# A list scheduler inside a kernel gets other numbers for its clock: engine overlap, bank release and matmul cadence in an attention and gated-unit kernel

## The chip, the core and the metric

The kernel runs on one core of one Trainium2 chip. The time is the device time of that core in microseconds, from the first to the last instruction and what lies around them; the document compares medians of several executions. The engines are called as the profile calls them: PE (TensorE matmul), PEld (its weight loads), DVE (VectorE), ACT (ScalarE), POOL (GpSimd), SP (SyncE, which issues most DMAs).

## What is computed

The input x has 2048 tokens of 576 features, in fp32. Cut to what matters:

```python
xn = _layernorm(x)
# A: attention, 32 heads of 18 features
qkv = xn @ wqkv;  q, k, v = per head
s = softmax(q @ k.T * 18 ** -0.5) @ v   # per head
s = concat(s) @ wo
# B: gated unit, 4608 columns, no nonlinearity inside
h = (xn @ w_gate) * (xn @ w_up)
g = silu(h @ w_down)
out = x + s * g
```

## The kernel before

**Three stages.** A first stage normalises x, turns it to columns and computes q, k and v. A main stage does the attention of all 32 heads and the gated unit at the same time. An end stage multiplies the attention output by wo, multiplies by the gate and adds x. The change touches the main stage only.

**Two halves of the array.** In the main stage PE's 128 rows are used as two halves of 64 rows that run different matmuls at once; the code calls them r = 0 and r = 1, and here they are half 0 and half 1. fp32 values are split into a high and a low part, so each product takes several matmuls. Five kinds of matmul are mixed:

- `a_item` (line 541), 64 per head, almost all on half 0: a 128x512 block of scores, written to one of two PSUM banks "a". DVE takes the row maximum of it (line 543). Below: an A.
- `b_item` (line 580), 64 per head, almost all on half 1: the block of scores again, transposed, with the maximum already inside, into one of two banks "b". ACT takes the exponential (line 582). Below: a B.
- `gu_op` (line 629): half 0 sums 27 matmuls into an up projection, which ACT copies out (line 636); half 1 sums 27 into a gate projection, which DVE multiplies by it (line 643). ACT and POOL then split the product (646, 653).
- `down_op` (line 677): half 0 puts three 128x288 matmuls into a bank, half 1 three more into the same bank, so the bank is handed over from one half to the other. DVE adds the sum to an accumulator (line 734), or ACT copies it out (728) and POOL adds it (697).
- `pv_group` (line 591): probabilities times v, in full fp32 over all 128 rows and four column strips. It needs both halves. It comes 96 times, three times a head, for 5, 5 and 6 blocks of tokens, and DVE or ACT empties its bank (597, 595). After a head's third group DVE finishes the head (`finish`, lines 605 to 609), and after every second head SP stores it (line 614).

Up, gate, down and `pv_group` share four banks "g". Below, a **stretch** is the work that both halves do between two `pv_group`s: 97 stretches in all. A half that has come to the end of its list in a stretch waits there for the other, since the next `pv_group` takes both.

**What sets the order.** Nothing in the order is decided at run time: each engine executes its instructions in the order in which they were written, and waits on semaphores where data or a bank is not ready. The order is made when the program is built, by the list scheduler `order()`. It keeps a clock per half (`clk`), the time from which each other engine is free (`free`, advanced by `engine()`), and the time from which each bank is free (`banks`). It takes the half whose clock is behind and issues an A or a B if its bank is free by this clock and its due time (`a_goal`, `b_goal`) has come, otherwise a down or an up or gate matmul whose data and bank are ready (`pick`, `can_go`). If nothing is ready it lets that half's clock run on by up to 0.3 and tries again; no instruction is written for such idle time. `visit()` writes a `pv_group` when enough exponentials are due and the two clocks stand within 0.04 of each other, or after 1.0 of waiting. The due times follow from `pace`, which is worked out from `part` and `span` ahead of the scheduler. `small()` slips in the splitting of weights, and the silu of finished tokens, when an engine is free.

Two details matter for the end of the main stage: the down matmuls of the last unit use a tile `wdl`, and `can_go` lets a unit's down matmuls begin only when `downed` of the unit before has passed, a time that `moved()` makes from the length of a DMA.

Of the kernel before, what the change touches and what calls it, by code (L numbers as in the profile page):

```python
# [40 lines left out]
def kernel(  # L41
# [456 lines left out]
    n = 8  # L498
# [24 lines left out]
    with ExitStack() as mid:  # L523
# [168 lines left out]
        def by_act(u, i):  # L692
            return i == 1 and u < len(units) - 1
# [117 lines left out]
        def stream(r, kind):  # L811

            def glu(n):
                c, q = units[n // 2]
                box = []
                for k in range(len(TERMS)):
                    def work(k=k):
                        if k == 0:
                            box.append(gu_start(r, n))
                        gu_op(r, n, box[0], k)  # L820
                        if q == NF2 - 1 and n % 2 and k % 3 == 2 and c < NCH - 1:
                            x_block(c + 1, k // 3, (64 * r,))
# [5 lines left out]
                    end = (("DVE", 0.70) if r else ("ACT", 0.60)) if k == len(TERMS) - 1 else None  # L828
                    yield 0.229, k == 0, work, end, ("g", n, k), len(TERMS)

            def down(u, n):
                own = alone(u, n)
                key = u, n, r * own
                s, i = divmod(n, 2)
                for k in range(len(DTERMS)):
# [7 lines left out]
                    if (own or r) and k == len(DTERMS) - 1:  # L843
                        end = ("ACT", 0.42) if by_act(u, i) else ("DVE", 0.46)
                    yield 0.131, (own or r == 0) and k == 0, work, end, ("d", u, 6 * n + k), len(DTERMS)
# [19 lines left out]
        turn = {"a": 0, "b": 0}  # L865

# [30 lines left out]
        def a_next(r=0):  # L897
# [10 lines left out]
            banks["a"][slot] = engine("DVE", clk[r] + 0.45, 0.70) + 0.18  # L908
            clk[r] += 0.229
# [10 lines left out]
        def b_next(r=1):  # L920
# [19 lines left out]
        KINDS = {"piece": ("ACT", 0.55), "big_piece": ("ACT", 0.71), "first": ("ACT", 0.70), "second": ("DVE", 0.45), "inverse": ("DVE", 1.06), "whole": ("ACT", 0.71)}  # L940
# [3 lines left out]
        def small(now):  # L944
# [6 lines left out]
            if q:  # L951
                name = q[0][0].__name__
                eng, length = KINDS.get(name, ("POOL", 0.0))
                if eng == "POOL" or free[eng] <= now + 0.1 + 0.15 * (now - quiet[0] if q is later else now - quiet[1]):
                    if eng != "POOL":
                        done = engine(eng, now, length)
                        if name in ("piece", "big_piece"):
                            engine("POOL", done + 0.1, 1.05 if name == "piece" else 1.47)
                    elif name in ("last", "rest"):
                        engine("POOL", now, 1.5 if name == "last" else 0.85)  # L960
# [6 lines left out]
        def rows(job):  # L967
# [4 lines left out]
            for r, tag in ((0, "a"), (1, "b")):  # L972
# [4 lines left out]
                banks[tag][slot] = done + 0.06  # L977
            rows_done[job[2]] = done + 6.0

        def visit(now):  # L980
# [15 lines left out]
            if many:  # L996
# [4 lines left out]
                end = engine("DVE", now + 0.2, 0.70) if ts[0] else engine("ACT", now + 0.2, 0.60)  # L1001
                banks["g"][k] = end + 0.06
# [46 lines left out]
        def late(goal, r=0):  # L1049
# [3 lines left out]
            fin = max(free["DVE"], clk[r] + 0.45) + 0.70  # L1053
# [31 lines left out]
        def order():  # L1085
# [5 lines left out]
            while going(0) or going(1) or na < TOTAL or nb < TOTAL or due or jobs:  # L1091
# [29 lines left out]
                elif op is not None:  # L1121
# [12 lines left out]
                    if kind == "d" and r == 0 and k % 6 == 5 and not own:  # L1134
                        handed[n, k // 6] = engine(eng, clk[0] + 0.35, 0.06) + 0.10
                        kept[n, k // 6] = slots[0, kind]
                    if end:
                        done = engine(end[0], clk[r] + 0.22, end[1])
                        banks["g"][kept.pop((n, k // 6)) if kind == "d" and not own else slots[r, kind]] = done + 0.06
# [7 lines left out]
                        else:  # L1147
                            gated[n] = done
                            fin = engine("ACT", done + 0.1, 0.63)
# [119 lines left out]
```

## Time and profile before

| | us |
|---|---|
| median of three executions (lowest, highest) | 2663.16 (2662.74, 2665.32) |
| the profiled execution: its own time | 2663.43 |
| the profiled execution: span of its instructions | 2661.7 |
| busy in the span: PE, PEld | 2634.4, 2148.6 |
| busy in the span: DVE, ACT, POOL | 1820.2, 1568.5, 663.9 |
| main stage: first A starts, last down matmul starts | 204.7, 2586.8 |

The profiled execution's own time is 1.7 us more than its span and 0.3 us more than the median. The granted PE clock was 0.999 of full speed over the span. How to read it: a PE that is busy 99% of the span says only that at least one of the two halves has a matmul in flight. A half that stands still while the other works is not seen as idle time in the profile's sums. It is seen in the timeline, where matmuls of each half can be told apart by their line (541 is half 0, 580 is half 1 outside the last 100 us), and by their number in a stretch.

### The profile page before, as it was taken

How to read it: one execution, taken by the hardware profiler on the slowest of the kernel's cores; microseconds unless marked ns; L12 is line 12 of the kernel's file. 1: busy time of each engine (PE TensorE's matmuls, PEld its weight loads, DVE VectorE, ACT ScalarE, POOL GpSimd, SP SyncE). 2: the span in 40 equal slices, each digit the busy share in tenths (PEclk: the TensorE clock that was granted, in tenths of full speed). 3: DMA queues.
4: the chain of work that ended last, by engine and by line, in shares of the span. 5: the costliest groups of instructions: out<-in, count | busy, mean ns of one | idle time of the engine just before them, and what ended most of it. 6: DMA issues, size and time to landing. Idle time of an engine off the chain costs nothing.

```text
span 2661.7 us, 59233 instructions
## 1 busy us (share of the span) xinstructions
PE 2634.4 (99%) x24504; PEld 2148.6 (81%) x24504; DVE 1820.2 (68%) x3007; ACT 1568.5 (59%) x3096; POOL 663.9 (25%) x683
## 2 busy tenths in 40 slices
PE   7999999999999999999999999999999999999999
PEld 6899887877877777787778788877878778877889
DVE  7208777766677777777777777777777778777226
ACT  4223667766766666666665666565665566665642
POOL 3114534444421211221111122211111121211125
PEclk9999999999999999999999999999999999999999
DMA  6799767658663434554454344454554353543356
GB/s 214 225 295 257 215 190 194 189 165 209 196 168 120 158 121 126 162 166 148 138 148 139 131 133 141 139 144 135 153 150 129 117 166 122 166 125 118 126 183 205
DMA packets 201581, 434.30 MB, mean 163 GB/s; under 512 B 81216, under 2 KB 130784, under 8 KB 167776
## 3 DMA queue, kind: packets, MB, share of 16 engines
q1 hardware_dynamic: 199072, 422.26, 53.3%
q0 software_dynamic: 2240, 8.26, 0.8%
q8 instruction: 192, 3.15, 0.5%
q14 instruction: 77, 0.63, 0.1%
HBM read 314.64 MB, written 110.56 MB: 160 GB/s over the span
## 4 chain that ended last, share of the span: by engine, by line
PE 97%; DVE 2%; DMA 1%; ACT 0%; POOL 0%; issue 0%; SPq 0%; POOLq 0%; ACTq 0%; DVEq 0%
PE pg L629 35%; PE pg L591 17%; PE pg L677 16%; PE pa L541 11%; PE pb L580 9%; PE pg L1226 2%; PE pg L393 2%; PE pa L336 2%; PE pb L336 2%; DVE xn L298 0%; DVE mx L543 0%; DVE st L287 0%; PE pb L1203 0%; DMA sqk<-hl 0%; PE pg L319 0%; DMA qs<-mr 0%
## 5 line engine op out<-in xcount | busy, mean ns | idle before, releaser
L543 DVE TENSOR_REDUCE mx<-pa 128x1 f32<-128x512 f32 x2048 | 1374.5, 687 | 288.8 <-PE pa L541 161.2
L582 ACT ACTIVATE pt<-pb 128x512 f32<-128x512 f32 x2048 | 1165.4, 597 | 506.0 <-PE pb L580 375.3
L629 PE MATMUL pg<-xc,wgu 64*128 64x512 f32 x7776 | 1444.1, 392 | 0.1
L629 PEld LDWEIGHTS pg<-xc,wgu 64*128 64x128 f32 x7776 | 1075.2, 186 | 68.0 <-issue 6.7
L677 PE MATMUL pg<-wd,hs 64*128 64x288 f32 x6816 | 854.9, 294 | 0.7 <-ACT st L728 0.7
L580 PE MATMUL pb<-qs,ks 56*128 56x512 f32 x2048 | 805.2, 401 | 0.4 <-DMA qs<-mr 0.3
L677 PEld LDWEIGHTS pg<-wd,hs 64*128 64x128 f32 x6816 | 790.6, 185 | 17.2 <-issue 2.5
L541 PE MATMUL pa<-ks,qs 54*128 54x512 f32 x2048 | 804.1, 401 | 0.0
L591 PE MATMUL pg<-pt,vt 128*32 128x512 f32 x4096 | 459.4, 594 | 3.4 <-DVE acc L734 1.8
L653 POOL TENSOR_TENSOR hs<-us,hs 128x512 fp32r<-128x512 f32 x144 | 186.0, 1291 | 1001.3 <-ACT hs L646 824.0
L541 PEld LDWEIGHTS pa<-ks,qs 54*128 54x128 f32 x2048 | 371.6, 184 | 76.9 <-issue 57.2
L580 PEld LDWEIGHTS pb<-qs,ks 56*128 56x128 f32 x2048 | 370.8, 184 | 13.2 <-issue 2.9
L697 POOL TENSOR_TENSOR acc<-acc,st 128x288 f32<-128x288 f32 x268 | 216.7, 810 | 560.3 <-ACT st L728 308.9
L591 PEld LDWEIGHTS pg<-pt,vt 128*32 128x32 f32 x4096 | 123.3, 110 | 282.9 <-issue 273.9
L597 DVE TENSOR_TENSOR oc<-oc,pg 128x512 f32<-128x512 f32 x64 | 44.0, 687 | 309.6 <-PE pg L591 309.6
L646 ACT ACTIVATE hs<-us 128x512 fp32r<-128x512 f32 x144 | 91.0, 632 | 117.5 <-DVE us L643 117.3
L208 POOL TENSOR_TENSOR wgu<-wraw,wgu 128x384 fp32r<-128x384 f32 x108 | 108.8, 1014 | 167.2 <-ACT wgu L207 138.2
L734 DVE TENSOR_TENSOR acc<-acc,pg 128x288 f32<-128x288 f32 x277 | 123.6, 447 | 35.5 <-PE pg L677 33.0
L643 DVE TENSOR_TENSOR us<-pg,us 128x512 f32<-128x512 f32 x144 | 98.5, 684 | 48.3 <-PE pg L629 39.1
L728 ACT ACTIVATE st<-pg 128x288 f32<-128x288 f32 x268 | 110.0, 411 | 29.3 <-PE pg L677 17.8
L636 ACT ACTIVATE us<-pg 128x512 f32<-128x512 f32 x144 | 86.0, 598 | 33.4 <-PE pg L629 18.9
L595 ACT ACTIVATE oc<-pg 128x512 f32<-128x512 f32 x32 | 19.2, 599 | 125.0 <-PE pg L591 125.0
(105 smaller groups left out, 1160.7 us busy)
## 6 DMA issues: line engine op xcount, KB each, us to landing
wgu<-swg SPq DMA_DIRECT2D x102, 1152.0 KB
wd<-swd SPq DMA_DIRECT2D x50, 1152.0 KB
swg<-wgu SPq DMA_DIRECT2D x36, 1152.0 KB
qs<-sqk SPq DMA_DIRECT2D x192, 144.0 KB
ks<-sqk SPq DMA_DIRECT2D x192, 144.0 KB
swd<-wd SPq DMA_DIRECT2D x18, 1152.0 KB
sqk<-hl SPq DMA_DIRECT2D x32, 512.0 KB
xc<-sx SPq DMA_DIRECT2D x48, 256.0 KB
```

The lines of the kernel that those rows point to most:

```text
L208: nc.gpsimd.tensor_tensor(w[:, 9 + b:12 + b, :], raw[:, b:b + 3, :], w[:, b:b + 3, :].bitcast(FT), op=OP.subtract)
L541: nc.tensor.matmul(p, q[rows, t * 128:(t + 1) * 128], k[rows, c * 512:(c + 1) * 512], start=True, stop=True)
L543: nc.vector.tensor_reduce(mx[h][:, t, c:c + 1], p, axis=AX.X, op=OP.max)
L580: nc.tensor.matmul(p, k[rows, t * 128:(t + 1) * 128], q[rows, c * 512:(c + 1) * 512], start=True, stop=True)
L582: nc.scalar.activation(pt[t, c // 2][:, c % 2, :], p, AF.Exp, scale=scale)
L591: nc.tensor.matmul(p[32 * c:32 * c + 32, :], vt[h // 2][:, t, 6 * (h % 2):6 * (h % 2) + 32], pt[t, c // 2][:, c % 2, :], start=t == ts[0], ...
L629: nc.tensor.matmul(ps, gw[n][half[r], a, :], xg[i][half[r], e, :], start=k == 0, stop=k == len(TERMS) - 1)
L653: nc.gpsimd.tensor_tensor(hj[:, 1, :], h32, hj[:, 0, :].bitcast(FT), op=OP.subtract)
L677: op = nc.tensor.matmul(ps[:, 0:HALF], hs[u][half[r], j, a, s * 128:(s + 1) * 128], dw[u][half[r], j, e, i * HALF:(i + 1) * HALF], start=( ...
L697: nc.gpsimd.tensor_tensor(a, a, st, op=OP.add)
L728: nc.scalar.activation(st, ps[:, 0:HALF], AF.Copy)
L734: nc.vector.tensor_tensor(a, a, ps[:, 0:HALF], op=OP.add)
```

## The change

The scheduler gets other numbers; no tile, no instruction and no DMA is added or taken away, and the due times (`part`, `span`, `pace`) keep their numbers. There are three kinds of edit:

- **Engines.** `engine()` still returns the end of an operation as start plus length, but the engine counts as free earlier than that: by 0.085 for DVE, 0.11 for ACT and 0.03 for POOL (not under 0.03 after the start).
- **Banks.** A bank counts as free 0.27 after the end of the operation that empties it for "a" and "b" (it was 0.18, and 0.06 after `max_rows`), and 0.20 for "g" (it was 0.06). A bank that is handed from half 0 to half 1 counts as handed 0.16 after the engine's notice (it was 0.10).
- **Durations.** A matmul of 512 columns counts 0.231 (0.229), one of 288 columns 0.132 (0.131); DVE and ACT operations count from nothing to 0.03 less, and begin 0.02 sooner after the matmul.

```diff
+        HIDDEN = {"DVE": 0.085, "ACT": 0.11, "POOL": 0.03}
+        SPARE, SPARE_G = 0.27, 0.20
...
         def engine(eng, start, length):
-            free[eng] = max(free[eng], start) + length
-            return free[eng]
+            start = max(free[eng], start)
+            free[eng] = start + max(length - HIDDEN[eng], 0.03)
+            return start + length
...
-            banks["a"][slot] = engine("DVE", clk[r] + 0.45, 0.70) + 0.18
-            clk[r] += 0.229
+            banks["a"][slot] = engine("DVE", clk[r] + 0.43, 0.685) + SPARE
+            clk[r] += 0.231
...
-            end = engine("ACT", clk[r] + 0.45, 0.60)
-            banks["b"][slot] = end + 0.18
-            clk[r] += 0.229
+            end = engine("ACT", clk[r] + 0.43, 0.596)
+            banks["b"][slot] = end + SPARE
+            clk[r] += 0.231
...
-                banks[tag][slot] = done + 0.06
+                banks[tag][slot] = done + SPARE
...
-                banks["g"][k] = end + 0.06
+                banks["g"][k] = end + SPARE_G
...
-                        handed[n, k // 6] = engine(eng, clk[0] + 0.35, 0.06) + 0.10
+                        handed[n, k // 6] = engine(eng, clk[0] + 0.33, 0.06) + 0.16
...
-                        done = engine(end[0], clk[r] + 0.22, end[1])
-                        banks["g"][kept.pop((n, k // 6)) if kind == "d" and not own else slots[r, kind]] = done + 0.06
+                        done = engine(end[0], clk[r] + 0.20, end[1])
+                        banks["g"][kept.pop((n, k // 6)) if kind == "d" and not own else slots[r, kind]] = done + SPARE_G
```

What it moves is seen only in the order that the scheduler then makes. Two places on PE follow. In the rows, line 541 is an A, 580 a B, 629 an up or gate matmul of either half, 677 a down matmul of either half, 591 a `pv_group`, and `x20` means 20 such rows in a row.

The first place is the end of the stretch ahead of the 29th `pv_group`, on PE. Before:

```order
L629 MATMUL pg<-xc,wgu 128x512
L541 MATMUL pa<-ks_1150,qs_1149 128x512
L629 MATMUL pg<-xc,wgu 128x512 x4
L580 MATMUL pb<-qs_1149,ks_1150 128x512
L629 MATMUL pg<-xc,wgu 128x512 x2
L541 MATMUL pa<-ks_1150,qs_1149 128x512
L580 MATMUL pb<-qs_1149,ks_1150 128x512
L629 MATMUL pg<-xc,wgu 128x512 x2
L541 MATMUL pa<-ks_1150,qs_1149 128x512
L580 MATMUL pb<-qs_1149,ks_1150 128x512
L629 MATMUL pg<-xc,wgu 128x512 x2
L591 MATMUL pg<-pt,vt 32x512 x20
```

Of the change, the same place:

```order
L580 MATMUL pb<-qs_1149,ks_1150 128x512
L541 MATMUL pa<-ks_1150,qs_1149 128x512
L629 MATMUL pg<-xc,wgu 128x512 x4
L580 MATMUL pb<-qs_1149,ks_1150 128x512
L629 MATMUL pg<-xc,wgu 128x512 x2
L541 MATMUL pa<-ks_1150,qs_1149 128x512
L629 MATMUL pg<-xc,wgu 128x512 x2
L580 MATMUL pb<-qs_1149,ks_1150 128x512
L629 MATMUL pg<-xc,wgu 128x512 x2
L591 MATMUL pg<-pt,vt 32x512 x20
```

In the rows of before, the last three A's follow each other on half 0, with no other matmul of half 0 between them and one up matmul behind; nearly all rows of line 629 there are gate matmuls of half 1. In the change each A has two or more up matmuls behind it on half 0. Counted over this whole stretch by the half that the built program gives each matmul, before has 40 matmuls of 512 columns (17 of them A's) and 12 of 288 on half 0, and 62 of 512 on half 1; the change has 67 of 512 on half 0 (19 of them A's), and 62 of 512 and 9 of 288 on half 1.

The second place is the end of the main stage on PE, from the last B's on. Before:

```order
L580 MATMUL pb<-qs_1149,ks_1150 128x512
L629 MATMUL pg<-xc,wgu 128x512 x2
L580 MATMUL pb<-qs_1149,ks_1150 128x512
L591 MATMUL pg<-pt,vt 32x512 x24
L677 MATMUL pg<-wd,hs 128x288 x84
L677 MATMUL pg<-wdl,hs 128x288 x96
L1203 MATMUL pb<-ident,oin 128x128 x4
```

Of the change:

```order
L677 MATMUL pg<-wd,hs 128x288 x2
L580 MATMUL pb<-qs_1149,ks_1150 128x512 x12
L677 MATMUL pg<-wdl,hs 128x288 x5
L580 MATMUL pb<-qs_1149,ks_1150 128x512
L677 MATMUL pg<-wdl,hs 128x288 x3
L580 MATMUL pb<-qs_1149,ks_1150 128x512
L677 MATMUL pg<-wdl,hs 128x288 x8
L580 MATMUL pb<-qs_1149,ks_1150 128x512
L677 MATMUL pg<-wdl,hs 128x288 x5
L580 MATMUL pb<-qs_1149,ks_1150 128x512
L677 MATMUL pg<-wdl,hs 128x288 x2
L591 MATMUL pg<-pt,vt 32x512 x24
```

Behind that last `pv_group` the change has one row more of the main stage, 73 matmuls of line 677, where before has 180; then the end stage begins in both. The last stretch ahead of a `pv_group` holds 23 B's in the change, 12 of them in one row, with matmuls of line 677 alone beside them; before has 22 B's there, spread among up and gate matmuls.

More of the change, by code (lines that the diff above doesn't have):

```diff
@@ L843, in down @@
                     if (own or r) and k == len(DTERMS) - 1:
-                        end = ("ACT", 0.42) if by_act(u, i) else ("DVE", 0.46)
-                    yield 0.131, (own or r == 0) and k == 0, work, end, ("d", u, 6 * n + k), len(DTERMS)
+                        end = ("ACT", 0.41) if by_act(u, i) else ("DVE", 0.45)
+                    yield 0.132, (own or r == 0) and k == 0, work, end, ("d", u, 6 * n + k), len(DTERMS)
             if kind == "g":
@@ L938, in b_next @@
                 due.append((h, i // 4, end + 0.1))
[L940 removed]
+        KINDS = {"piece": ("ACT", 0.52), "big_piece": ("ACT", 0.68), "first": ("ACT", 0.70), "second": ("DVE", 0.45), "inverse": ("DVE", 1.05), "whole": ("ACT", 0.68)}
         quiet = [0.0, 0.0]
@@ L1000, in visit @@
                 pv_group(h, ts, k)
-                end = engine("DVE", now + 0.2, 0.70) if ts[0] else engine("ACT", now + 0.2, 0.60)
-                banks["g"][k] = end + 0.06
+                end = engine("DVE", now + 0.2, 0.687) if ts[0] else engine("ACT", now + 0.2, 0.598)
+                banks["g"][k] = end + SPARE_G
                 if ts[-1] == NT - 1:
```

10 lines of the change are left out of this document (5 added, 5 removed).

## The prediction

> **What bounds the kernel now.** The page first: the busy times, and the chain of work that ended last.
>
> ```profile
> PE 2634.4 (99%) x24504; PEld 2148.6 (81%) x24504; DVE 1820.2 (68%) x3007; ACT 1568.5 (59%) x3096; POOL 663.9 (25%) x683
> PE 97%; DVE 2%; DMA 1%; ACT 0%; POOL 0%; issue 0%; SPq 0%; POOLq 0%; ACTq 0%; DVEq 0%
> ```
>
> PE carries the chain, and no other engine is busy for more than 68%. But 99% hides the question that matters here: are both halves of the array working, or only one? For that I compare the main stage with the work in it. The groups of the page give the counts, the view of single lines gives the stage's first and last matmul (column "first and last start"):
>
> ```profile
> L629 PE MATMUL pg<-xc,wgu 64*128 64x512 f32 x7776 | 1444.1, 392 | 0.1
> L677 PE MATMUL pg<-wd,hs 64*128 64x288 f32 x6816 | 854.9, 294 | 0.7 <-ACT st L728 0.7
> L580 PE MATMUL pb<-qs,ks 56*128 56x512 f32 x2048 | 805.2, 401 | 0.4 <-DMA qs<-mr 0.3
> L541 PE MATMUL pa<-ks,qs 54*128 54x512 f32 x2048 | 804.1, 401 | 0.0
> L591 PE MATMUL pg<-pt,vt 128*32 128x512 f32 x4096 | 459.4, 594 | 3.4 <-DVE acc L734 1.8
> ...
> L541 PE MATMUL pa<-ks,qs x2048: 385/393/503, 204.7 to 2466.9; 54*128 54x512 f32 x187
> ...
> L677 PE MATMUL pg<-wdl,hs x96: 287/292/397, 2579.2 to 2586.8; 64*128 64x288 f32 x96
> ```
>
> A duration of 392 ns is a matmul's passage through the array, not its pace. The pace of a half is read from the timeline. Between two B's on half 1 stand two gate matmuls, the other two of the four being up matmuls on half 0:
>
> ```profile
> 974.63 0.39 PE L580 MATMUL pb<-qs,ks 56*128 56x512 f32 x1
> 974.83 0.65 PE L629 MATMUL pg<-xc,wgu 64*128 64x512 f32 x4
> 975.31 0.39 PE L541 MATMUL pa<-ks,qs 54*128 54x512 f32 x1
> 975.33 0.39 PE L580 MATMUL pb<-qs,ks 56*128 56x512 f32 x1
> ```
>
> 975.33 - 974.63 = 0.70 for three, so 0.233 for a matmul of 512 columns. For 288 columns two neighbours on one half stand 0.14 apart in the rows below (981.35 and 981.49); I take 0.133, which fits all such neighbours best.
>
> The even share of a half is then (7776 + 2048 + 2048) / 2 x 0.233 = 1383.1 plus (6816 + 96) / 2 x 0.133 = 459.6, together 1842.7. The stage lasts 2586.8 - 204.7 = 2382.1, of which `pv_group`s take 459.4. The 97 stretches between them thus last 1922.7, **80.0 more than the work of an even share**. That, 3% of the kernel, is all that a better order can win.
>
> Where do the 80.0 go? Giving each matmul its half as the built program has it, and the two paces above, the longer half of each stretch adds up to 1888.3 over the 97 stretches. So 1888.3 - 1842.7 = 45.6 is one half waiting at a `pv_group` for the other, because the lists are uneven. The remaining 34.4, or 0.35 per stretch, is refilling the array behind a `pv_group` and waits that hold the longer half.
>
> One stretch shows how an uneven list arises, the one whose end front rows show (970.3 to 986.0). PE, then DVE:
>
> ```profile
> 981.35 0.29 PE L677 MATMUL pg<-wd,hs 64*128 64x288 f32 x1
> 981.36 0.39 PE L629 MATMUL pg<-xc,wgu 64*128 64x512 f32 x1
> 981.49 0.29 PE L677 MATMUL pg<-wd,hs 64*128 64x288 f32 x1
> 981.59 0.39 PE L580 MATMUL pb<-qs,ks 56*128 56x512 f32 x1
> 981.64 0.50 PE L541 MATMUL pa<-ks,qs 54*128 54x512 f32 x1
> 981.83 1.32 PE L629 MATMUL pg<-xc,wgu 64*128 64x512 f32 x5
> 982.95 0.50 PE L541 MATMUL pa<-ks,qs 54*128 54x512 f32 x1
> 982.99 0.40 PE L580 MATMUL pb<-qs,ks 56*128 56x512 f32 x1
> 983.23 0.63 PE L629 MATMUL pg<-xc,wgu 64*128 64x512 f32 x2
> 983.55 0.50 PE L541 MATMUL pa<-ks,qs 54*128 54x512 f32 x1
> ...
> 985.98 1.06 PE L591 MATMUL pg<-pt,vt 128*32 128x512 f32 x8 [0.95 <-DVE us L643]
> ```
>
> ```profile
> 982.21 1.28 DVE L543 TENSOR_REDUCE mx<-pa 128x1 f32<-128x512 f32 x2
> ```
>
> Half 0 issues A's at 981.64, 982.95 and 983.55, one up matmul more, and then nothing until 985.98, over two us. Half 1 meanwhile works through its gate matmuls. The list gave half 0 40 x 0.233 + 12 x 0.133 = 10.9 and half 1 62 x 0.233 = 14.4, and the stretch lasted 985.98 - 970.34 = 15.6. The scheduler had let half 0's clock run on, since by its own clock a bank or DVE was not yet free, and had put nothing into that time.
>
> **The change part by part.** No instruction is added, so the sum is made of what the new order does.
>
> *The engines' overlap.* Were the numbers of before wrong? The DVE row above holds two reduces in 1.28; one takes 0.687 (its group on the page, in the next rows), so the second began 1.28 - 0.687 = 0.59 after the first. The old clock counted 0.70, the new one 0.685 - 0.085 = 0.60. For ACT two exponentials that follow closely, and one that waited for its B:
>
> ```profile
> L543 DVE TENSOR_REDUCE mx<-pa 128x1 f32<-128x512 f32 x2048 | 1374.5, 687 | 288.8 <-PE pa L541 161.2
> L582 ACT ACTIVATE pt<-pb 128x512 f32<-128x512 f32 x2048 | 1165.4, 597 | 506.0 <-PE pb L580 375.3
> ...
> 970.97 1.08 ACT L582 ACTIVATE pt<-pb 128x512 f32<-128x512 f32 x2
> 971.83 0.39 PE L580 MATMUL pb<-qs,ks 56*128 56x512 f32 x1
> 972.27 4.78 ACT L582 ACTIVATE pt<-pb 128x512 f32<-128x512 f32 x7 [0.23 <-PE pb L580]
> ```
>
> 1.08 - 0.597 = 0.48 from start to start; the old clock counted 0.60, the new one 0.49. From a B to its exponential 972.27 - 971.83 = 0.44; the new clock has 0.43. So the new clock tells truer when an engine can take the next A or B, and idles less.
>
> [...]
>
> *The banks.* A stalled A follows its bank's release closely: the first reduce of the pair ends at 982.21 + 0.687 = 982.90, and the A of 982.95 takes that bank 0.05 later. The new clock wants 0.27 between them. From an A to the next use of its bank the old clock counted 0.45 + 0.70 + 0.18 = 1.33 and the new one counts 0.43 + 0.685 + 0.27 = 1.385: A's are spaced 0.055 wider where the bank decides, and 0.10 closer where DVE does. What the wider spacing buys is that an A less often reaches PE's queue ahead of its bank. I count nothing for it, bounded by zero and the whole 34.4 of the waits.
>
> *The paces.* 0.231 and 0.132 for 0.229 and 0.131 cost nothing by themselves: they are nearer to 0.233 and 0.133.
>
> *The sum of the order.* Counted in the same way, with the same paces, the change's longer halves add up to 1864.7 over 97 stretches. The 96 `pv_group`s keep their sizes. **1864.7 - 1888.3 = -23.6.** In the stretch shown, half 0 now has 67 x 0.233 = 15.6 and half 1 62 x 0.233 + 9 x 0.133 = 15.6.
>
> *What is late next: the end.* The front rows show that in the change 23 B's stand in the last stretch ahead of the last `pv_group`, with down matmuls alone beside them, 7.6 us of work for the longer half. There the two banks "b" decide: 0.44 + 0.597 + 0.05 = 1.09 a bank, 0.545 for a B, 23 x 0.545 = 12.5. ACT alone would allow 23 x 0.48 = 11.0. I take 12.5 less 7.6 and the usual 0.35: **+4.5**; bounds 3 (ACT's 11.0 alone) and 7 (0.65 for a B, if a bank stays shut for the 0.27 that the new clock wants instead of 0.05).
>
> Behind the last `pv_group` before has 180 down matmuls, the change 73 (43 on the longer half, 43 x 0.133 = 5.7). In before they cover the finish of the last head:
>
> ```profile
> 2572.91 14.23 PE pg L677 x179
> ...
> 2575.27 1.96 SPq L614 DMA_DIRECT2D so<-ot  x4
> 2577.34 3.93 SPq L1170 DMA_DIRECT2D oin<-so  x4
> 2581.16 0.26 ACT L1195 ACTIVATE oin<-oin 128x64 f32<-128x64 f32 x1 [0.76 <-DMA oin<-so]
> 2587.07 0.66 PE L1203 MATMUL pb<-ident,oin 128*128 128x128 f32 x4
> ```
>
> DVE finishes the head, SP stores it, and loads it again; the first tile stands at 2581.16 + 0.26 = 2581.4, which is 8.5 after the `pv_group` ended at 2572.9. Before, PE reached the transposes at 2587.07 anyway. In the change only 5.7 of the 8.5 is covered: **+2.8** (bounds 0, if the store and load run quicker on emptier DMA queues, and 5). SP's order of issues around it is the same in both.
>
> *Sum*: -23.6 + 4.5 + 2.8 = -16.3 against the profiled execution's own 2663.4 (span 2661.7 and 1.7 around it), 2647.1. The median of the runs is 0.3 less. I predict **2647**.
>
> **The rivals.**
>
> *The waits go too.* The truer clock also spares the longer half part of its 34.4. For it speaks that in the change only 35 A's stand less than 1.3 us of work behind the last A but one, which has the same bank, where before has 83. Against it: many of these A's stood on the half that idled anyway. If a third goes, 11 us: 2636.
>
> *The waits come out (slower).* The B of 982.99 starts right behind the stalled A of 982.95, on the other half: a wait on one half can hold up both. In before a wait often fell on a half that had time to spare. With even lists each wait pushes the `pv_group` back. If all 80.0 stay, the order wins nothing and the end costs its 7.3: 2671. It decides slower from the point where the loss per stretch beyond the longer half grows from 0.35 to over 0.35 + (16.3 / 97) = 0.52. Against it speaks an even stretch of before, between these two `pv_group`s:
>
> ```profile
> 330.63 4.43 PE pg L591 x40
> 359.60 5.29 PE pg L591 x48
> ```
>
> It lasted 359.60 - 335.06 = 24.5 with lists of 24.15 on both halves: 0.4 lost, no more than the average.
>
> *The overlap does not hold.* Reduces 0.687 apart would make each of the A's that the clock puts closer than 1.4 us to the last but one late by some 0.17 (2 x 0.687 against 2 x 0.60). By the order these are some 500 A's, 85 us: up to 2732. The same hardware took about 600 such A's in before, and the 1.28 row contradicts it. I give it almost nothing. [...]
>
> *Nothing of note.* Half of the balance is lost to waits and the end costs its bounds: about 2660.
>
> **How the numbers follow.** Forecast 0.60; waits go too 0.20; nothing of note 0.09; waits come out 0.10; no overlap 0.01. The range must leave out at most 0.2: 2630 (the first rival with half of the waits gone, 17 us) to 2661. A change below 0.2%, 5.3 us, is about what a measurement of this kernel can't tell from none: faster is under 2658, and takes the forecast and the first rival, 0.80; within 0.2% 0.09; slower 0.11.
>
> **What would show it.** Right: the last start of line 677 about 16 to 20 us sooner, PE's groups with the same counts, the stretch ahead of the 29th `pv_group` with up matmuls of half 0 behind every A; at the end a row of B's about 0.5 apart, and idle PE of some 3 us ahead of the transposes of line 1206, which is line 1203 before. Wrong: the stage as long as before with fewer gaps at `pv_group`s and more inside (waits come out), or reduces 0.687 apart.

## The result and the profile after

| | before | change |
|---|---|---|
| median of 20 runs each, us | 2663.82 | 2666.49 |
| lowest, highest | 2662.60, 2668.17 | 2664.52, 2672.25 |
| profiled execution: time, span | 2663.43, 2661.7 | 2665.97, 2664.2 |
| main stage (first A to last down matmul) | 2382.1 | 2383.0 |
| from there to the end of the span | 74.8 | 76.7 |
| granted PE clock | 0.999 | 0.996 |

The ratio of change to before is **1.0011, 95% interval [1.0005, 1.0017]**: no gain, if anything 0.1% slower. The forecast of 2647 and its range were wrong.

The page and the view of single lines of the change, in the same places as the prediction's rows of before:

```profile
PE 2624.0 (98%) x24504; PEld 2131.9 (80%) x24504; DVE 1810.2 (68%) x3007; ACT 1551.3 (58%) x3096; POOL 662.0 (25%) x683
PE 91%; DMA 3%; DVE 2%; SPq 1%; ACT 1%; POOL 1%; issue 1%; POOLq 0%; ACTq 0%; DVEq 0%
L629 PE MATMUL pg<-xc,wgu 64*128 64x512 f32 x7776 | 1383.4, 392 | 6.1 <-DMA xc<-sx 4.2
```

```profile
L541 PE MATMUL pa<-ks,qs x2048: 384/393/625, 204.5 to 2478.7; 54*128 54x512 f32 x187
L677 PE MATMUL pg<-wdl,hs x96: 286/292/605, 2569.5 to 2587.5; 64*128 64x288 f32 x96
```

The last start of line 677, foretold 16 to 20 us sooner, is 0.7 later. PE is busy for 10.4 us less in a span that is 2.5 longer, the chain now has 3% of DMA in it, and line 629 waited 4.2 us for a DMA, which it did not before. The longest passages, 0.625 and 0.605 where 0.393 and 0.292 are usual, point to a lower clock in places.

**Did the balance come?** The stretch ahead of the 29th `pv_group`, again its end and the `pv_group`s around it, PE:

```profile
964.44 4.50 PE L591 MATMUL pg<-pt,vt 128*32 128x512 f32 x40
...
982.91 0.39 PE L541 MATMUL pa<-ks,qs 54*128 54x512 f32 x1
982.91 0.86 PE L629 MATMUL pg<-xc,wgu 64*128 64x512 f32 x4
983.38 0.39 PE L580 MATMUL pb<-qs,ks 56*128 56x512 f32 x1
983.61 0.40 PE L629 MATMUL pg<-xc,wgu 64*128 64x512 f32 x2
983.87 0.50 PE L541 MATMUL pa<-ks,qs 54*128 54x512 f32 x1
983.87 0.73 PE L629 MATMUL pg<-xc,wgu 64*128 64x512 f32 x2
984.22 0.39 PE L580 MATMUL pb<-qs,ks 56*128 56x512 f32 x1
984.45 0.40 PE L629 MATMUL pg<-xc,wgu 64*128 64x512 f32 x2
984.77 0.64 PE L591 MATMUL pg<-pt,vt 128*32 128x512 f32 x4
```

Yes. Both halves issue to the end, and no half stands still for two us. The lists are 15.6 on both halves, and the stretch, from 968.87 to 984.77, lasts 15.9: 0.3 lost, within the usual 0.35 that the prediction carried over.

**Where it went.** Each stretch is now counted from its first matmul to the `pv_group` behind it, less the prediction's two paces on its longer half: the loss beyond the longer half. (By this count before has 41.1, not 34.4, since the 6.7 us between the `pv_group`s' busy time, 459.4, and their starts, 452.7, falls to the stretches.) The stretches are numbered from 0 to 96; the one shown is number 28.

| us | longer halves | lost, all | 0 | 1-18 | 19 | 20-94 | 95 | 96 |
|---|---|---|---|---|---|---|---|---|
| before | 1888.3 | 41.1 | 2.7 | 8.4 | 0.3 | 28.4 | 0.1 | 1.2 |
| change | 1864.7 | 65.0 | 5.2 | 12.8 | 7.3 | 28.3 | 9.8 | 1.4 |
| difference | -23.6 | +23.9 | +2.5 | +4.4 | +7.0 | -0.1 | +9.7 | +0.2 |

With 0.6 more for the `pv_group`s, 1.9 more in the end stage and a main stage that begins 0.2 sooner, -23.6 + 23.9 + 0.6 + 1.9 - 0.2 = +2.6, against 2.5 in the spans. Taken together, the 75 stretches from 20 to 94 wait no longer than in before. Two stretches, 19 and 95, cost 16.7 of the 23.9.

**Stretch 95**, the row of B's at the end. PE, then windows of the same place (PE's busy time, then PEclk, the granted clock, and behind it the DMA share):

```profile
2562.30 0.50 PE L580 MATMUL pb<-qs,ks 56*128 56x512 f32 x1 [0.20 <-ACT pt L582]
2563.09 0.99 PE L580 MATMUL pb<-qs,ks 56*128 56x512 f32 x2 [0.29 <-ACT pt L582]
2564.27 1.00 PE L580 MATMUL pb<-qs,ks 56*128 56x512 f32 x2 [0.19 <-ACT pt L582]
2565.45 1.29 PE L580 MATMUL pb<-qs,ks 56*128 56x512 f32 x2 [0.19 <-ACT pt L582]
2566.90 1.32 PE L580 MATMUL pb<-qs,ks 56*128 56x512 f32 x2 [0.16 <-ACT pt L582]
2568.38 1.32 PE L580 MATMUL pb<-qs,ks 56*128 56x512 f32 x2 [0.16 <-ACT pt L582]
...
2574.38 6.01 PE L591 MATMUL pg<-pt,vt 128*32 128x512 f32 x48
2580.32 7.45 PE L677 MATMUL pg<-wdl,hs 64*128 64x288 f32 x73
2588.93 0.66 PE L1206 MATMUL pb<-ident,oin 128*128 128x128 f32 x4 [1.15 <-DMA oin<-so]
```

```profile
2556.00:2562.00 6.00, 6.00 (x56) 4.68 (x48) 1.60 (x3) 3.95 (x8) 0.80 (x1) 1.00 0.00 0
2562.00:2568.00 6.00, 4.97 (x10) 2.03 (x9) 0.00 (x0) 5.12 (x11) 0.80 (x1) 0.79 0.00 0
2568.00:2575.00 7.00, 6.84 (x34) 5.47 (x37) 0.00 (x0) 4.37 (x8) 0.00 (x0) 0.50 0.00 0
```

The B's come in pairs, each pair waiting for the exponential that empties its bank. At full clock the pairs stand 1.18 apart, 0.59 a B; the forecast had 0.545. Then the clock falls to 0.50, the passages grow from 0.4 to 0.6 and the pairs stand 1.45 and 1.48 apart, 0.74 a B. The low clock lasts into the `pv_group`, which takes 6.01 instead of the 5.36 that one of 48 usually takes. The profile shows ten matmuls in the six us in which it fell. All 23 B's at 0.59 would take 13.6 us; the stretch lasted 17.4, so by this estimate some 4 of the 9.8 lost came with the low clock.

**Stretch 19**, from 745.63 on. PE:

```profile
757.22 0.39 PE L541 MATMUL pa<-ks,qs 54*128 54x512 f32 x1
761.54 1.65 PE L629 MATMUL pg<-xc,wgu 64*128 64x512 f32 x6 [3.94 <-DMA xc<-sx]
...
764.27 0.62 PE L629 MATMUL pg<-xc,wgu 64*128 64x512 f32 x1
```

SP's queue at that place of the change, then of before (issues of one kind that follow each other are one row; its second number runs from the start of the first to the end of the last):

```profile
739.25 0.90 SPq L529 DMA_DIRECT2D vt<-sv  x1
740.25 5.62 SPq L359 DMA_DIRECT2D xc<-sx  x2
745.91 0.86 SPq L259 DMA_DIRECT2D qs<-sqk  x2
...
749.11 3.35 SPq L614 DMA_DIRECT2D so<-ot  x4
753.40 4.76 SPq L359 DMA_DIRECT2D xc<-sx  x4
```

```profile
726.80 4.32 SPq L359 DMA_DIRECT2D xc<-sx  x6
731.55 1.83 SPq L356 DMA_DIRECT2D xc<-sx  x2
734.12 4.60 SPq L359 DMA_DIRECT2D xc<-sx  x4
739.22 1.57 SPq L356 DMA_DIRECT2D xc<-sx  x2
740.93 5.49 SPq L359 DMA_DIRECT2D xc<-sx  x6
...
756.37 2.19 SPq L529 DMA_DIRECT2D vt<-sv  x1
```

Here the tokens' columns, xc, are replaced for the second quarter of the tokens. Before, these loads had SP to themselves, and the v load vt<-sv came behind them. In the change the v load, the loads of q and k and four stores of two finished heads stand ahead of most of them; the second xc load is issued 5 us after the first, and most follow from 753.4 on, 4 us before PE stops at 757.6.

The new order also leaves these loads less room, since a block of xc can be replaced only when the old one has been read for the last time. With the halves taken from the built program, half 1 starts its last matmul on the first old block at 746.7 in the change; the load that replaces this block is issued at 756.34, and half 1 is due to use it when PE stops at 757.6. In before these three are 728.3, 729.26 and 750.7, because a `pv_group`, down matmuls, A's and B's stand between the last gate matmul on the old columns and the first on the new. So there were 22 us of room before and 11 in the change, and of the eleven nearly ten had passed when SP, behind its other work and one more xc load, came to issue the load.

PE then stands still for 3.94 us, and behind it runs at a lower clock: 0.62 for a passage, and in windows:

```profile
757.00:761.00 4.00, 0.61 (x6) 0.27 (x4) 1.26 (x2) 0.95 (x3) 1.82 (x2) 0.86 0.90 212
761.00:767.00 6.00, 5.46 (x32) 5.18 (x34) 2.10 (x5) 1.33 (x3) 0.00 (x0) 0.53 1.05 236
```

So a wait of 3.9 costs 7. The Trainium skill, "TensorE: Matmul & The Clock Gate", Part 1, says that the array goes back to half its clock after an idle window of about 3.4 us. The 0.53 behind a wait of 3.94 fits that, but the start of the fall does not come 3.4 us after the last matmul: if the clock halves, the 0.86 of the window 757 to 761 means 1.1 us at half clock, so it fell at about 759.9, 2.3 us into the wait.

### The profile page after: what moved, and what is told of

It is laid out like the page before. It is cut to its first block, busy times and chain, and to the rows that moved or that the text cites. A ratio compares the mean times of both kernels' runs of the same rounds, so it can differ in the third digit from the quotient of the medians.

```text
span 2664.2 us, 59222 instructions
## 1 busy us (share of the span) xinstructions
PE 2624.0 (98%) x24504; PEld 2131.9 (80%) x24504; DVE 1810.2 (68%) x3007; ACT 1551.3 (58%) x3096; POOL 662.0 (25%) x683
## 4 chain that ended last, share of the span: by engine, by line
PE 91%; DMA 3%; DVE 2%; SPq 1%; ACT 1%; POOL 1%; issue 1%; POOLq 0%; ACTq 0%; DVEq 0%
PE pg L629 33%; PE pg L591 17%; PE pg L677 15%; PE pa L541 11%; PE pb L580 9%; PE pg L1229 2%; PE pa L336 1%; PE pg L393 1%; PE pb L336 1%; DMA xc<-sx 1%; DMA ks<-sqk 1%; SPq L425 1%; DVE mx L543 0%; ACT pt L582 0%; POOL wgu L208 0%
## 5 line engine op out<-in xcount | busy, mean ns | idle before, releaser
L629 PE MATMUL pg<-xc,wgu 64*128 64x512 f32 x7776 | 1383.4, 392 | 6.1 <-DMA xc<-sx 4.2
L629 PEld LDWEIGHTS pg<-xc,wgu 64*128 64x128 f32 x7776 | 1043.3, 186 | 70.8 <-issue 5.1
L677 PE MATMUL pg<-wd,hs 64*128 64x288 f32 x6816 | 815.0, 294 | 1.2 <-POOL hs L653 1.0
L677 PEld LDWEIGHTS pg<-wd,hs 64*128 64x128 f32 x6816 | 764.7, 186 | 14.8 <-issue 3.4
```

Source lines behind the costliest of these rows:

```text
L629: nc.tensor.matmul(ps, gw[n][half[r], a, :], xg[i][half[r], e, :], start=k == 0, stop=k == len(TERMS) - 1)
L677: op = nc.tensor.matmul(ps[:, 0:HALF], hs[u][half[r], j, a, s * 128:(s + 1) * 128], dw[u][half[r], j, e, i * HALF:(i + 1) * HALF], start=( ...
```

## The experiments

The ratios are those to the kernel before on the same chip, with the 95% interval. "Lost" is the loss beyond the longer half, as above.

**e1: the v load.** Meant to move the v load from ahead of xc to the 49th B of its head:

```diff
-            if i == 16 and h % 2 == 0 and h // 2 + 1 < H // 2:
+            if i == (48 if h == 8 else 16) and h % 2 == 0 and h // 2 + 1 < H // 2:
```

> The change, with one DMA moved: the load of v for heads 10 and 11 (vt<-sv) is issued at the 49th B of head 8 instead of the 17th, so that it no longer stands just ahead of the loads of the second x block (xc<-sx) in SP's queue. The order on PE, DVE, ACT and POOL stays that of the change. Theory of places (the even lists win their 23.6 us, and three places give it back, one of them the stretch from 745.6 in which PE waits 3.9 us for xc): that stretch, 25.6 us in the change, falls to about 19, and the kernel to about 2660 (6 us under the change, 0.9985 of before). Theory that waits come out everywhere once the lists are even: the stall there is one wait among many, the time given back turns up in later stretches, and the kernel stays at 2666. If the store of the finished heads and the loads of q and k ahead in SP's queue are what delays xc, the stretch also stays at 25.

2667.30, ratio 1.0011 [1.0002, 1.0020]; 8.0 lost in stretch 19. The edit took the wrong load: the one ahead of xc is issued by head 6, not 8. So it tells nothing of its question and is in effect a repeat of the change. As such it is useful: 12.8 lost in stretches 1 to 18, 29.8 in 20 to 94 and 9.8 in 95, against 12.8, 28.3 and 9.8. The losses belong to the order and are not noise, except in stretch 0 (3.7 here, 5.2 in the change).

**e2: work beside the B's.** The last unit's down matmuls no longer wait in the scheduler for the DMA behind the unit before:

```diff
-                                downed[n] = moved(clk[r] + 0.3, 1.18) if (n + 1) % NF2 else 0.0
+                                downed[n] = moved(clk[r] + 0.3, 1.18) if (n + 1) % NF2 and n < len(units) - 2 else 0.0
```

> The change, but the scheduler no longer waits for a DMA between the last unit but one and the last (downed of unit 70 is its end, not its end plus some 7 us). The order is that of the change until there; then the 96 down matmuls of the last unit are written beside the last B's instead of behind them, and none is left behind the last pv_group. Theory of places: the 9.8 us that the stretch ahead of the last pv_group loses to B's in a row fall to about 1, the stretch takes about 14 (23 B's at 0.59), but the finish of the last head (some 8.5 us from the pv_group's end to the first transposes) has no cover at all. From 17.4 + 7.2 + 1.5 to about 14 + 8.5: 2 to 4 us under the change, 2663. If the uncovered finish also lowers PE's clock in the end stage, no gain or 2 us slower. Theory that waits come out everywhere: no change outside, the same here.

2664.82, ratio 1.0003 [0.9994, 1.0012]. The gain is the one expected, 2 to 4 us under the change's order (e1, 2667.30 on the same chip), though the two intervals overlap. The loss in stretch 95 fell from 9.8 to 1.5, and the main stage, which here ends with a `pv_group`, by 10.9 to 2372.1; but the end stage grew by 9.6 to 86.3. All down matmuls now stood ahead of the last `pv_group` and nothing was left behind it. The waits of PE:

```profile
PE pb L1206 <- DMA oin<-so: 9.0, 1, 9.0
```

That is the finish of the last head that the prediction put at 8.5, wholly uncovered. The end needs its down matmuls in both places.

**e3: another pace.** `PACE` 0.995 for 1.005, which makes the whole order anew:

> The change with PACE 0.995 instead of 1.005: A's and B's fall due 1% sooner, so the last B's stand beside up and gate matmuls, with 16.5 us of work on the longer half and 23 B's in the last stretch, and about 30 us of up, gate and down matmuls stand behind the last pv_group. The whole order is made anew; its longer halves add up to 1869.6 (change 1864.7, before 1888.3). Theory of places: the end gives back nothing (change: about 12 us for the B's in a row, the slower clock behind them and the uncovered finish), so 12 less and 5 more than the change, 2659, or 2653 if the stall at xc happens not to arise in this order. Theory that waits come out everywhere: 2664 to 2668, with 10 us or more of additional waits spread over the stretches.

2670.48, ratio 1.0023 [1.0014, 1.0032]. Stretches 19 and 95 were healed (1.1 and 0.4), the end stage was as before (74.8), the longer halves 1869.6. But stretches 1 to 18 lost 18.3, and 7.9 came in one new place, stretch 36. ACT and PE there:

```profile
1178.70 0.68 ACT L791 ACTIVATE wor<-wor 128x576 fp32r<-128x576 f32 x1 [5.91 <-DMA wor<-in_A_wo_dram]
```

```profile
1179.92 0.79 PE L580 MATMUL pb<-qs,ks 56*128 56x512 f32 x1 [5.48 <-ACT pt L582]
```

A small conversion of weights of wo, put into ACT's order before its load had landed, held the exponentials queued behind it, and so the B's. The time is over both that were expected. The places that stall are those of the order, and a new order has new ones.

**e4 and e8: the change without the overlap, and without the later bank releases.** The other edits stay:

```diff
-        HIDDEN = {"DVE": 0.085, "ACT": 0.11, "POOL": 0.03}
+        HIDDEN = {"DVE": 0.0, "ACT": 0.0, "POOL": 0.0}
```

> The change without the engines' overlap: HIDDEN is 0 for DVE, ACT and POOL; banks, paces and durations are the new ones. The longer halves of its order add up to 1886.0, so the even lists of the change (1864.7) come from the overlap alone. Theory of places: this order has neither the 23.6 nor the B's in a row at the end, so it is about as fast as before, 2660 to 2666, with the waits beyond the longer half at 35 to 42 us as in before (41 by the same count) and not 65 as in the change. Theory that the later release of banks by itself removes waits: they fall to 30 or less, and the kernel to 2655 or less.

```diff
-        SPARE, SPARE_G = 0.27, 0.20
+        SPARE, SPARE_G = 0.18, 0.06
...
-                banks[tag][slot] = done + SPARE
+                banks[tag][slot] = done + 0.06
...
-                        handed[n, k // 6] = engine(eng, clk[0] + 0.33, 0.06) + 0.16
+                        handed[n, k // 6] = engine(eng, clk[0] + 0.33, 0.06) + 0.10
```

> The change with the old release of banks (0.18 and 0.06 instead of 0.27 and 0.20, 0.10 instead of 0.16 at the hand-over); overlap, paces and durations are the new ones. Its longer halves add up to 1872.8 and its last stretch has 23 B's beside 8.2 us of work, as in the change. If the later release spares waits, the stretches 36 to 94 lose more beyond the longer half than the 22.5 us of the change (35 or so) and the kernel takes 2675 to 2685. If it does not, they lose 20 to 25, and the kernel takes about 8 more than the change for its less even lists, less whatever one stall like that at xc is worth: 2667 to 2675.

e4 2670.70, 1.0025 [1.0016, 1.0033]; e8 2685.89, 1.0076 [1.0062, 1.0090]. e4 met neither of its theories: 49.3 lost, and nearly 5 us over the range of the first. e8 is 1 us over the range of its first one, and it has stalls of its own at xc: 9.0 lost in stretch 19 and 5.1 in stretch 70.

**e10 and e11: the durations alone, and the banks alone.** e10 has both edits of e4 and e8. e11 is the kernel before with releases at 0.27 and 0.20 and the hand-over at 0.16.

> Of the change only the new durations, paces and the start: the overlap at 0 and the old bank releases and hand-over. Longer halves come to 1890.4 us (before 1888.3). If the bank releases carry the gain in balance (the change without them was 22 us slower than before, the change without the overlap 7), the durations alone do nothing for the balance: 2662 to 2668, 41 to 50 us lost beyond the longer halves. If the durations by themselves disturb the order (as the early stretches of e4 suggest, 10.6 against 8.4), over 2670.

> Of the change only the later release of the banks (0.27, 0.20) and the later hand-over; old durations, no overlap. Longer halves come to 1895.5 us by count (before 1888.3), so the balance gets worse by 7.2. If the later release spares waits of its own (the change without it lost 7 to 14 us more beyond the longer halves than with it), the loss falls from 41 to some 34 and the time stays about 2664. If it spares none, 2671. If it is enough by itself, under 2658.

e10 2686.09, 1.0091 [1.0076, 1.0106]; e11 2690.89, 1.0100 [1.0086, 1.0114]. e11 is 20 us over the highest time that was expected. For e10 the second theory came out, over 2670. The six orders together:

| kernel | durations | overlap | banks | longer halves | lost | ratio |
|---|---|---|---|---|---|---|
| before | | | | 1888.3 | 41.1 | 1 |
| e10 | yes | | | 1890.4 | 59.2 | 1.0091 |
| e11 | | | yes | 1895.5 | 61.3 | 1.0100 |
| e8 | yes | yes | | 1872.8 | 71.5 | 1.0076 |
| e4 | yes | | yes | 1886.0 | 49.3 | 1.0025 |
| change | yes | yes | yes | 1864.7 | 65.0 | 1.0011 |

The overlap carries the balance: -17.6 in e8 against e10, -21.3 in the change against e4. The bank releases, which I had counted at nothing, are worth 17 us by the ratios, 19 by the medians, beside the other two edits (e8 against the change) and cost 27 by themselves. Of that gain 8.1 is balance and 6.5 less loss; how much of it is the releases' own and how much the chance of a new order is not shown. And every new order loses more beyond its longer halves than before, 8 to 30 us. In the stretch where e10 and e11 each lose most (5.4 and 9.3), PE waits for a DMA. A row of each, PE:

```profile
2019.04 0.73 PE L629 MATMUL pg<-xc,wgu 64*128 64x512 f32 x4 [1.31 <-DMA xc<-sx]
```

```profile
2596.89 9.63 PE L677 MATMUL pg<-wd,hs 64*128 64x288 f32 x93 [4.24 <-DMA wd<-swd]
```

**e5, e6, e7: the two places repaired, apart and together.** e5 moves the right v load, that of head 6. e6 lets the last A's come due sooner, so that A's and B's end earlier beside up and gate matmuls:

```diff
-            if i == 16 and h % 2 == 0 and h // 2 + 1 < H // 2:
+            if i == (48 if h == 6 else 16) and h % 2 == 0 and h // 2 + 1 < H // 2:
```

```diff
-            return QUICK * i if i < N else QUICK * N + pace * (i - N)
+            return QUICK * i if i < N else QUICK * N + pace * (i - N) - 0.04 * max(0, i - 1700)
```

> The change, with the load of v that stands right ahead of the loads of the second x block in SP's queue moved: it is the one issued in head 6 (e1_vt moved head 8's, which stood elsewhere), now at the 49th B instead of the 17th. The order of the other engines stays. Theory that this load is what holds up xc (the first xc issue behind it took 4.98 us, the others about 0.5): the stretch from 745 falls from about 25.6 to 19 to 20, and the kernel by 5 to 7 us to about 2660. Theory that SP's queue as a whole is what holds it up (loads of q and k, store of a head): 0 to 2 us.

> The change, with the A's from the 1701st of 2048 on due 0.04 us sooner each (the B's follow), and everything before in the order of the change. The longer halves add up to 1864.4 (change 1864.7); in the last stretch 23 B's stand beside 16.1 us of work instead of 7.6, and 13 us of down matmuls stand behind the last pv_group instead of 5.7. Theory of places: the last stretch loses about 0.3 instead of 9.8, PE's clock stays full there, the finish of the last head is covered: 10 to 12 us under the change, 2655. Theory that waits come out everywhere: the waits appear in the stretches from the 1700th A on, and the kernel gains under 4.

> Both e5_vt6 and e6_ramp. Theory of places: the two add up, 16 to 18 us under the change, 2649, faster than before by 0.5%: the even lists of the change would then have been worth what they count, less some 7 us of waits in the first stretches. Theory that waits come out everywhere: 2660 or more.

e5 2664.71, 1.0005 [0.9996, 1.0014]; e6 2659.39, 0.9984 [0.9975, 0.9993]; e7 2658.00, 0.9976 [0.9966, 0.9986]. e6 did at the end what it should: 0.1 lost in stretch 95, the same longer halves (1864.4), the usual 28 to 29 in 20 to 94, and the main stage 9.7 shorter than the change's; its median, 7 under the change's, falls short of the 10 to 12 expected. Its last `pv_group` and first transposes:

```profile
2556.96 5.36 PE L591 MATMUL pg<-pt,vt 128*32 128x512 f32 x48
...
2570.70 7.56 PE L677 MATMUL pg<-wdl,hs 64*128 64x288 f32 x93
2580.17 0.66 PE L1206 MATMUL pb<-ident,oin 128*128 128x128 f32 x4 [1.92 <-DMA oin<-so]
```

In e5 and e7 stretch 19 still lost 5.7 and 5.8: the v load was worth some 2 us of it, as the second theory of e5 had it, and e7 is faster than before but not by the 0.5% expected.

**e9: the stores too.** e7, and the store of the finished heads 4 and 5 from POOL's queue:

```diff
-                    nc.sync.dma_start(
+                    (nc.gpsimd if g == 2 else nc.sync).dma_start(
```

> The change with three edits: the A's due sooner from the 1701st on (as in e6), the v load of head 6 at the 49th B (as in e7), and the store so<-ot of heads 4 and 5 issued from POOL's queue, not SP's. If those stores ahead of xc in SP's queue are what is left of the stall in stretch 19 (5.8 us lost there in e7, 0.3 before the change), the stretch falls to about 2 and the time from e7's 2658 to about 2654. If xc is late for another reason (its own transfers), the stretch stays at 5 to 6 and the time at 2658. If POOL's queue delays the store past the down projection that reads it, a wait turns up further back and the time is over 2660.

**2654.05, 0.9963 [0.9951, 0.9976]**: the best of all, 10.3 us under before. Stretch 19 lost 3.7; PE waits three times for xc there, 1.6 us in all, and the clock stays whole:

```profile
757.00:761.00 4.00, 3.45 (x35) 2.92 (x33) 2.55 (x6) 2.05 (x5) 2.08 (x2) 1.00 0.95 233
761.00:767.00 6.00, 4.92 (x43) 3.85 (x41) 3.26 (x7) 3.23 (x8) 0.56 (x1) 1.00 1.02 240
```

The DMA share, 0.95 and 1.02, says that the 16 DMA engines are full there, so an earlier issue alone would not bring xc much sooner. But they were as full in before (1.01 to 1.05 from 727 to 748), which lost nothing; it had 22 us of room, and e9 has 11. Room is not all of it either: where before goes on to the third quarter of the tokens it has 10.2 on half 1 and loses 0.1. What the rest of the stall is was not tested. (e9's profiled span is 2654.5 and e7's 2654.6, and the intervals of the two overlap. That stretch 19 fell from 5.8 to 3.7 is in the traces; that e9 is faster than e7 as a whole is not shown.)

**e12: a still later release.** e9 with 0.35 for 0.27 in `SPARE`:

> The best version so far (e9) with the banks a and b free 0.35 after their engine, not 0.27. Longer halves come to 1878.8 us, 14.4 more than e9's 1864.4. If the order's balance decides and the waits stay at e9's 54.7, the time is 2654 + 14 = 2668. If a longer lead buys waits as the step from 0.18 to 0.27 did, some of the 14 comes back: 2658 to 2662. At 2654 or below, waits would count for as much as the balance.

2671.66, 1.0028 [1.0017, 1.0039]. Longer halves +14.4, lost 60.4 against e9's 54.7. A longer lead spares no waits here; the time rose by the balance and some more.

**e13, e14, e15: the weights' stores.** In the change SP stood, ahead of xc, up to 15.3 us at a store that waits for POOL's splitting (SP's waits from 712 to 757 us, times and longest):

```profile
SPq L214 <- POOL wgu L208: 19.9, 2, 15.3
SPq L245 <- POOL wd L240: 7.0, 1, 7.0
```

So I took those stores out of SP's queue: e13 in the change, e14 in e9, e15 in before.

```diff
-            nc.sync.dma_start(swg[f], w.bitcast(FT))
+            nc.gpsimd.dma_start(swg[f], w.bitcast(FT))
...
-            nc.sync.dma_start(swd[p], w.bitcast(FT))
+            nc.gpsimd.dma_start(swd[p], w.bitcast(FT))
```

> The change with the stores of the split weights (swg<-wgu and swd<-wd) issued from POOL's queue, behind the splits that they wait for, and not from SP's; the order of every engine's arithmetic stays. If SP's wait for POOL's splits holds up xc, the loads of stretch 19 go out some 13 us sooner, the stretch falls from 7 to 8 us lost to under 1, and the time from 2666.5 to about 2659. If the v load ahead of them or the transfers themselves are the cause, the stretch stays at 5 or more and the time at 2664 to 2667. If the early stretches lose to SP as well, their 12.8 falls towards 8.4 and the time to 2655.

> e9's kernel with the stores of the split weights on POOL's queue as well. If SP's wait is the cause, the 3.7 us still lost in stretch 19 go to under 1 and the time from 2654 to about 2651. If not, it stays at 2654. If POOL is late with its products because it now issues 54 stores more, 2656 or over.

> The kernel before with the same two kinds of stores on POOL's queue. It lost 0.3 us in stretch 19 and 8.4 in 1 to 18, so by the theory that the stores hold up xc only in the change's order there is nothing to win: 2662 to 2666. If emptier SP queues help any order, it gains as much as the change does, 4 to 8 us.

2684.57, 1.0073 [1.0058, 1.0088]; 2666.41, 1.0015 [1.0006, 1.0023]; 2672.48, 1.0038 [1.0026, 1.0050]. Stretch 19 lost 8.0 in e13 and 3.8 in e14, no less than without the edit. That alone does not refute the theory, for the edit did not free SP: it only waits one row further on, at the raw load into the buffer that POOL is still splitting (e13, 700 to 765 us), and PE's wait is there again:

```profile
SPq L137 <- POOL wd L240: 34.8, 2, 28.3
```

```profile
776.88 1.65 PE L629 MATMUL pg<-xc,wgu 64*128 64x512 f32 x6 [4.55 <-DMA xc<-sx]
```

What speaks against the theory is when the first xc load may go. Half 0 starts its last matmul on the first old block at 739.7 in the change and at 754.5 in e13, and the load is issued at 740.25 and 754.88, right behind it; SP's wait for POOL was over by then. The 13 us could not have been won in either kernel.

And every kernel with the edit is slower, most of it early: 11.6 and 11.4 lost in stretch 0 of e13 and e15 (5.2 and 2.7 without the edit), 19.9 in 1 to 18 of e13 and e14 (12.8 and 13.0). Stores on POOL's queue are not free for this kernel: e14 landed in the range foreseen for a late POOL, and nothing over 2666 was expected of e15.

## Why the prediction was wrong, point by point

- **What bounds the kernel** was right as far as it went: 80.0 us above the work of an even share, 45.6 of them imbalance.
- **The order's -23.6** was right as a count of the built program, and the runs bear it out in stretches 20 to 94: the loss beyond the longer half stayed the same there (28.4 and 28.3), so the time followed the count.
- **The truer clock** was right in kind: without the overlap the longer halves are 21.3 longer (e4). In time e4 is only 3 to 4 us slower than the change, and their intervals touch. **"I count nothing for it"**, of the banks, was wrong as a price: without them the change is 17 to 19 us slower (e8).
- **The end, +4.5 and +2.8**, was mis-sized. Measured are +9.7 in stretch 95, +0.6 on the `pv_group` behind it and +1.9 at the transposes: 12.2 against 7.3. The +2.8 held nearly: the transposes begin 8.5 after the `pv_group` has ended (2588.93 - 2580.39), as foretold, only the down matmuls between them covered more of it. The +4.5 assumed 0.545 a B at full clock. It is 0.59, and 0.74 when the clock has fallen. The upper bound, 7, was too low for the same reason: no rate in it knew of the clock.
- **The step that failed most** is that the sum was closed with the end: "what is late next" was asked there alone, and all else beyond the longer half was taken over from before unchanged. That left out +7.0 at xc, +4.4 in stretches 1 to 18 and +2.5 in stretch 0, 14 us in other places. "SP's order of issues around it is the same in both" was said of the end of the main stage and asked nowhere else. At xc it does not hold, and PE wants the new columns 11 us after it has let go of the old ones, not 22; no term of the sum asked when data has to be there.
- **The rivals.** "The waits come out" gave 2671 and was nearest in time, but by luck: its mechanism is refuted for the 75 stretches from 20 to 94, where even lists kept their gain. What came out was a few single stalls, of which two make up most; only the +4.4 in stretches 1 to 18, spread over several of them, could still be this rival: from 305 to 745 us PE's stops for ACT and DVE add up to 4.8 in the change and to 1.3 in before. "The overlap does not hold" is refuted: the reduces still follow each other 0.58 apart, as in this row of the change's DVE, 1.27 less the 0.686 of one:

```profile
983.14 1.27 DVE L543 TENSOR_REDUCE mx<-pa 128x1 f32<-128x512 f32 x2
```

- **Open** stay which of the order's moves brought the +4.4 in stretches 1 to 18, what is left of stretch 19 in e9 (3.4 us over before's), and why the durations alone cost 22 us. The variation of stretch 0 (3.7 to 5.2 in the change's own order: e1, e2, e5 and the change) says that more than half of its +2.5 may be chance. The three repairs of e9 gave 9.7 of span against the change, and no kernel reached the forecast's 16.3 under before.

## What to carry to other kernels

Count of an order what it fills, and then walk along every queue for what it moved: here the balance came as counted in 75 stretches, and most of it was lost in two places that no count of matmuls shows, a row of operations that starve PE, and loads that were wanted sooner and stood behind others in SP's queue. When the tables of a scheduler change, the whole order is made anew, and its single stalls with it: of the orders tried here each lost 8 to 30 us more beyond its longer halves than the order of before, so such a change should be charged for new stalls until they have been looked for. And edits of such a table are not to be judged one by one: the durations alone, the banks alone and the overlap without the banks were each 0.8 to 1.0% slower, and all three together 0.1%.

## What the runs showed of the hardware that was not expected

- PE's clock falls even though PE never stops for long. In the row of B's the gaps before a pair are 0.16 to 0.29 us and the profile has PE busy for 4.97 of 6 us, yet the granted clock averages 0.79 in those six and 0.50 in the next seven, and a matmul of 512 columns takes 0.6 instead of 0.4. In e6, where the same B's stand among other matmuls, it stays at 1.00. So the profile's busy time does not tell when the clock will fall.
- A stop of 3.94 us cost nearly twice its length, 7 us; the clock averages 0.53 from 761 to 767, behind it.
- DMA issues on POOL's queue hold up POOL's arithmetic, though POOL is busy for a quarter of the span. In e15 a store begins 0.30 behind the split ahead of it and takes 0.57, so the product behind it starts 0.9 us after the split; in before it follows the split at once. Between 100 and 320 us of e15 PE waited for such a product, for which it did not wait before. The issue accounts for 0.9 of this wait; the rest is open:

```profile
PE pg L677 <- POOL hs L653: 3.8, 1, 3.8
```
